# Ten units of the second filter group ahead of the mixer, and its later steps on an even grid

## The chip, the cores and the metric

The kernel runs on one core of one Trainium2 chip. The metric is the device time of one execution in microseconds (us), taken as the median over runs.

## The reference, cut to what matters

The input `x` has 8 batches of 3008 rows and 256 channels, in fp32. A filter is applied to every channel by a Fourier transform along the rows, and a token and channel mixer follows:

```python
X = np.fft.rfft(x, axis=1)
Y = X * (filt_r + 1j * filt_i)[None, :, :]
x = np.fft.irfft(Y, n=3008, axis=1)
h = np.maximum(x.transpose(0, 2, 1) @ w_tok1, 0.0) @ w_tok2     # 3008 -> 256 -> 3008
u = x + h.transpose(0, 2, 1)
out = u + np.maximum(u @ w_ch1, 0.0) @ w_ch2                    # 256 -> 1536 -> 256
```

The four mixer weights arrive as 64-bit floats and are converted on the chip.

## The kernel before, in words

The length 3008 is 47 x 64, so the Fourier transform is done as matmuls of length 64, a stage of length 47 with the filter in between, and the inverse.

**The filter.** `dft(bs)` is a generator for a group of batches; every `next()` puts one small piece of work into the program. The groups are `((0,), (1, 2), (3, 4), (5, 6), (7,))`. A group's steps are, in order:

- One step that only loads x tiles ahead (not in the first group). `x_load` (L397) fetches a tile of 128 partitions x 2 x 256 with two DMAs on SP's queue. From the second group on the tiles come from a pool of two buffers, `xp`.
- The length-64 units, `a_unit` (L415): 12 per batch, so 24 for a group of two. Each is a matmul of 128x512 (run as two passes, L417), a copy by ScalarE into `t1` (L422, two buffers) and a DMA of 256 KB to `z_tmp` on ScalarE's queue (L423). Behind each unit the load of the tile two units later is put into the program. In the first group the result stays on the chip: it is copied into `turned` (L419), and 16 VectorE transposes (L455) then turn its rows.
- Two steps without computation. The first of them loads the first chunks of `z_tmp` (`t2_load`, L457), filter and tables (`w_load`).
- The 33 length-47 steps (L515 on). Step k runs `b_unit(k)` (a matmul, L470, then the filter's products on VectorE, L482 to L486) and `bi_unit(k - 1)` (a matmul with the products, L494, a copy, L500, and after each second one a DMA to `g_tmp`, L505). For the first group, `filt_double` (L223) copies half of a filter tile on ScalarE, and `b_unit` reads it.

A unit's or step's PSUM bank is one of two, `acc` and `b`, taken by `free_bank`; the mixer's token sums and `u_part` use the same two.

**The weights.** `convert()` (L384) advances three queues over a list of weight tiles: the DMA of one tile, a ScalarE pass of the one before, and VectorE (or VectorE and PE, L284 and L285) for the one before that.

**The mixer.** `mix` (L703) goes over 8 batches x 36 items (6 column blocks m of 512 x 6 parts jp). In each item it runs the up matmuls (`up_first` L597, `up_last` L613), VectorE sums, the down matmuls of the item before (L631), and yields at three places, 0, 1 and 2. Items with jp 3 and 4 also run a `u_part` of the next block (L557, L562), between places 1 and 2. After each block, `finish` puts VectorE sums into the next items; they fall into items with i % 6 of 0, 1 and 2. Item 32 holds the token sums of the next batch (L540), which read `g_tmp` through `t4` (L534).

**The order.** It is written out by hand: every engine works through its own instructions in the order of the program, and SP and ScalarE also issue DMAs in that order. The first group's filter runs first, with conversions between its steps. The second group's generator (`second`) is advanced five times before the first mixer: once at the first group's step k == 25 (only x loads), twice in the loop over the remaining conversions, and twice right before `mix`. Its remaining steps are put at the places of the first mixer's 36 items by the condition at L835: while length-64 units remain, at places 1 and 2 of items 0 to 3 and at all three places from item 4 on; afterwards at place 1 of every item and at place 2 of odd ones. Later groups use place 1 alone. When the group ends (`done`), the loads of the next batch's `t4` go out.

Of the kernel before, what the change touches and what calls it, by code (L numbers as in the profile page):

```python
# [24 lines left out]
K2 = 32  # L25
# [4 lines left out]
NXC = A // XC  # L30
# [15 lines left out]
PARTS = (0, 64, 112)  # L46
BY_PE = 6
EARLY = 12
GROUPS = ((0,), (1, 2), (3, 4), (5, 6), (7,))


# [73 lines left out]
def kernel(  # L125
# [49 lines left out]
    def bank(tag):  # L175
        return (psg if tag == "pg" else psum).tile([P, 512], FP32, tag=tag, name="ps_" + tag)
# [114 lines left out]
    def w1_load(i):  # L291
        st = stage(512)
        rows = moe_w_tok1.rearrange("(n2 n1) t -> n2 n1 t", n1=N1)
        q = nc.sync if i < EARLY else nc.gpsimd
        last = 2 * i + 2 == A
# [88 lines left out]
    def convert():  # L384

        ended[0] += 1
        while behind and behind[0][0] < ended[0] - 2:
            behind.pop(0)[1]()
        advance(end)
        advance(copy)  # L390
        advance(begin)
# [139 lines left out]
    def t4_load(b, c, lo=PARTS[0], hi=P):  # L531
        if lo == 0:
            t4[b, c] = t4p.tile([P, TC4, D], FP32, tag="t4", name="t4")
        nc.sync.dma_start(t4[b, c][lo:hi], rows_of(g_d, b)[lo:hi, ts(c, TC4), :])  # L534
# [9 lines left out]
    def token_relu(acc):  # L544
        h1 = h1p.tile([P, TC, D], FP32, tag="h1", name="h1")
        nc.scalar.activation(out=h1, in_=acc, func=AF.Relu)
        return h1

    def width(m):
        return 512 if m < MT - 1 else 448  # L550
# [37 lines left out]
    def h_sums(hh, t, w):  # L588

        h = hh[:, :, 0:w // 2]  # L590
        return sums(t[:, :, 0:w // 2], h[:, 1:3], h[:, 0:2], h[:, 0], h[:, 3])

    def up_first(jp, ut, vt, w, g):
        hw = w // 2
        for ps, n, mov in ((g[0][:, 0], 0, ut[:, 0, 0:hw]), (g[0][:, 1], 5, vt[:, 2, 0:hw]),
                           (g[1][:, 0], 6, vt[:, 0, 0:hw]), (g[1][:, 1], 4, vt[:, 1, 0:hw])):
            nc.tensor.matmul(ps[:, 0:hw], chan[0][:, jp, n, :], mov, start=True, stop=True)  # L597

        s = sp.tile([P, 3, 256], FP32, tag="s", name="s")[:, :, 0:hw]
        nc.scalar.copy(out=s[:, 0], in_=g[0][:, 0, 0:hw])  # L600
        return s

    def up_middle(hh, w, g, s):
        hw = w // 2
        u2 = hh[:, 2, 0:hw]
        v(u2, g[0][:, 1, 0:hw], s[:, 0])
        v(s[:, 1:3], g[1][:, :, 0:hw], u2.unsqueeze(1).to_broadcast([P, 2, hw]))
# [74 lines left out]
    def u_part(b, m, dh):  # L682
        if dh == 0:
            uts[b, m] = up.tile([P, DH, 512], FP32, tag="u", name="u")
        u_unit(b, m, h1s[b], uts[b, m], dh)
# [13 lines left out]
    def one_step():  # L699
        if todo_v:  # L700
            todo_v.pop(0)()

    def mix(next_ready):  # L703

        wait = []
        pos, hhs, tts = {}, {}, {}

        def loads(b):
            if b + 1 < B and next_ready(b):
                for c in wait:  # L710
                    t4_load(b + 1, c)
                wait.clear()

        items = [(b, m, jp) for b in range(B) for m in range(MT) for jp in range(JP)]
        n = MT * JP
        for i in range(len(items) + 1):
            now, old = i < len(items), i >= 1
            convert()
            if now:
                b, m, jp = items[i]  # L720
                if i % n == 0:
                    wait.append(0)
                w = width(m)
                hhs[i] = hp.tile([P, 4, 256], FP32, tag="hh", name="hh")
                g = [bank("pg").rearrange("p (s n) -> p s n", s=2) for _ in range(2)]
                s = up_first(jp, uts[b, m], vts[b, m], w, g)
                up_middle(hhs[i], w, g, s)
            one_step()
            if old:
                bo, mo, jo = items[i - 1]  # L730
                tts[i - 1] = tp.tile([P, 4, 256], FP32, tag="t", name="t")
                for f in h_sums(hhs[i - 1], tts[i - 1], width(mo)):
                    f()
                down(mo, jo, 0, hhs[i - 1], tts[i - 1], pos.setdefault((bo, mo), []))
            yield b, i % n, 0
            convert()
            if now:
                up_last(jp, uts[b, m], vts[b, m], w, g, s, hhs[i])
            one_step()
            loads(b)  # L740
            yield b, i % n, 1
            if old:
                down(mo, jo, 1, hhs.pop(i - 1), tts.pop(i - 1), pos[bo, mo])
                if jo == JP - 1:
                    todo_v.extend(finish(bo, mo, uts[bo, mo], pos[bo, mo]))
                    one_step()
                    one_step()
            if now:
                if m + 1 < MT and jp in (3, 4):
                    u_part(b, m + 1, jp - 3)  # L750
                    if jp == 4:
                        wait.append(m + 1)
                        todo_v.extend(v_steps(b, m + 1))
                if b + 1 < B:
                    j = i % n - n
                    if j == -4:
                        h1s[b + 1] = token_relu(token_sums(b + 1))
                    elif j == -3 or j == -2:
                        u_part(b + 1, 0, j + 3)
                        if j == -2:  # L760
                            todo_v.extend(v_steps(b + 1, 0))
            loads(b)
            yield b, i % n, 2
        while todo_v:
            one_step()

    with tc.manual_schedule():
        nc.sync.dma_start(wa0, wa0_d)
        nc.vector.memset(turned[:, A:K2, :], 0.0)
        for t in filts:  # L770
            nc.vector.memset(t, 0.0)
        rounds = 0
        second = dft(GROUPS[1])
        for i, _ in enumerate(dft(GROUPS[0])):
            if i == 0:
                for t, src in ((wai_t, wait_d), (wa, wa_d), (wai, wai_d), (ident, ident_d)):
                    nc.scalar.dma_start(t, src)

            if i < NXC:
                if i in (0, 2, 4, 6):  # L780
                    advance(begin)
                if i == 5:
                    advance(copy)
                if i in (7, 9, 11):
                    convert()
                    rounds += 1
            else:
                if (i - NXC) % 3 == 2:
                    convert()
                    rounds += 1  # L790

                k = i - NXC - 2
                if 19 <= k < 25:
                    t4_load(0, k - 19, 0, PARTS[1])
                elif k == 25:
                    next(second)
                elif k in (30, 31):
                    for c in range(3):
                        t4_load(0, 3 * (k - 30) + c, PARTS[1], PARTS[2])
        for c in range(A // TC4):  # L800
            t4_load(0, c, PARTS[2], P)
        sum_up()
        both = wcp.tile([P, 2, JP, 7, P], FP32, tag="wc", name="wc")

        chan.extend((both[:, 0], both[:, 1]))
        for i in range(rounds, A // 2 + TC * N2 // NG):
            convert()
            if i - rounds < XB:
                next(second)
            if i == A // 2 + BY_PE - 1:  # L810
                sum_up()
                acc = token_sums(0)
        h1s[0] = token_relu(acc)
        for dh in range(DH):
            convert()
            u_part(0, 0, dh)
        for f in v_steps(0, 0):
            f()
        for _ in range(XB):
            next(second)  # L820
        group, todo, done = -1, iter(()), True

        def next_ready(b):
            return done or b != GROUPS[group][-1]

        for b, i, place in mix(next_ready):
            if group + 1 < len(GROUPS) and b == GROUPS[group + 1][0]:
                if not done:
                    raise AssertionError("the filter's steps don't fit beside the mixer's")
                group += 1  # L830
                done = group + 1 == len(GROUPS)
                todo = iter(()) if done else dft(GROUPS[group + 1]) if group else second
                spread = True

            if not done and (place == 1 or group == 0 and (spread and (place == 2 or i > 3) or place == 2 and i % 2)):  # L835
                spread = next(todo, "end")
                done = spread == "end"

# [29 lines left out]
```

## Time and profile before

| | |
|---|---|
| Median of 6 runs | 2587.64 us (2586.78 to 2590.57) |
| Profiled execution | 2589.03 us |
| Its span | 2587.0 us |
| PE, matmuls | 2505.7 us busy, 97% |
| VectorE (DVE) | 1815.3 us, 70% |
| ScalarE (ACT) | 691.1 us, 27% |
| GpSimd (POOL) | 526.7 us, 20% |
| DMA | 205.20 MB, mean 79 GB/s |

The page lists busy time by engine, then 40 slices of the span in which a digit is the busy share in tenths, then DMA queues, the chain of waits that ended last, and the costliest groups of instructions. In the timeline a row is: start, duration, engine, line, operation, output<-inputs, count, and in brackets the idle time of the engine before it with what ended it. `SPq` and `ACTq` are the queues that issue DMAs. PE is the matmul engine, PEld its weight loads. In the windows view each row is a stretch of time with the busy time of every engine in it.

### The profile page before, as it was taken

The page shows a single profiled execution, that of the slowest core. Times are in us where ns is not written, and L with a number is a line of the kernel's source. Part 1 is how long each engine was busy: PE and PEld are TensorE (multiplying, and loading weights), DVE is VectorE, ACT ScalarE, POOL GpSimd, SP SyncE. Part 2 cuts the span into 40 slices and gives each one's busy share as a digit, 9 for nine tenths or more (in the row PEclk, how much of TensorE's full clock was granted, in tenths as well). Part 3 has the DMA queues.
Part 4 walks back from the last instruction along what each step waited for, and adds up shares of the span by engine and source line. Part 5 has one row for each costly group of instructions (what it writes and reads, how often), then busy time and mean ns, then how long its engine had stood idle before and what let it go on. Part 6 is the DMA issues. An engine that isn't in the chain of part 4 may idle for free.

```text
span 2587.0 us, 31459 instructions
## 1 busy us (share of the span) xinstructions
PE 2505.7 (97%) x10952; PEld 2001.9 (77%) x10952; DVE 1815.3 (70%) x3458; ACT 691.1 (27%) x1347; POOL 526.7 (20%) x966
## 2 busy tenths in 40 slices
PE   5979999999999999999999999999999999999998
PEld 2556766788878777888787777788888888888887
DVE  6897888556675888746666788846678577647676
ACT  2433222123221222222321222212222122212222
POOL 3653211111211112112112111121121121211212
PEclk7999999999999999999999999999999999999999
DMA  6964333312232332202232223211232121100001
GB/s 167 232 195 154 109 106 103 106 48 90 90 90 63 88 88 72 80 17 89 90 96 77 75 84 87 80 31 57 90 85 75 50 64 53 25 9 8 17 12 21
DMA packets 151835, 205.20 MB, mean 79 GB/s; under 512 B 34217, under 2 KB 102035, under 8 KB 151677
## 3 DMA queue, kind: packets, MB, share of 16 engines
q1 hardware_dynamic: 81068, 115.65, 15.3%
q0 software_dynamic: 30656, 39.93, 6.4%
q10 hardware_dynamic: 39952, 47.61, 5.7%
q8 instruction: 87, 1.43, 0.2%
q14 instruction: 72, 0.58, 0.1%
HBM read 131.23 MB, written 71.83 MB: 78 GB/s over the span
## 4 chain that ended last, share of the span: by engine, by line
PE 80%; DVE 12%; DMA 2%; issue 2%; ACT 2%; POOL 0%; SPq 0%; ACTq 0%; DVEq 0%; POOLq 0%
PE ps_po L631 27%; PE ps_pg L597 16%; PE ps_pg L613 12%; PE ps_b L540 4%; PE ps_b L557 4%; DVE t L575 2%; PE ps_acc L540 2%; PE ps_acc L557 2%; DVE hh L575 2%; PE ps_acc L494 2%; PE ps_b L562 2%; PE ps_acc L417 2%; PE ps_b L470 1%; DVE u L575 1%; PE ps_b L494 1%
## 5 line engine op out<-in xcount | busy, mean ns | idle before, releaser
L575 DVE TENSOR_TENSOR hh<-ps_pg,s 128x512 f32<-128x512 f32 (+3 forms) x864 | 482.0, 585 | 624.4 <-ACT s L600 623.8
L676 POOL DMA_DIRECT2D out_dram<-r x757 | 409.8, 550 | 1948.4 <-ACT hh L618 928.3
L618 ACT ACTIVATE hh<-hh 128x512 f32<-128x512 f32 (+1 forms) x576 | 347.9, 621 | 1121.4 <-DVE hh L575 1121.4
L631 PE MATMUL ps_po<-t,wc 128*128 128x256 f32 (+1 forms) x2304 | 535.5, 375 | 5.3 <-DVE t L575 4.6
L631 PEld LDWEIGHTS ps_po<-t,wc 128*128 128x128 f32 x2304 | 434.5, 190 | 132.8 <-issue 53.3
L631 PE MATMUL ps_po<-hh,wc 128*128 128x256 f32 (+1 forms) x1728 | 413.2, 375 | 2.9 <-POOL wc L339 2.5
L597 PE MATMUL ps_pg<-v,wc 128*128 128x256 f32 (+1 forms) x1728 | 413.4, 375 | 0.3
L631 PEld LDWEIGHTS ps_po<-hh,wc 128*128 128x128 f32 x1728 | 327.5, 190 | 41.8 <-POOL wc L339 2.9
L597 PEld LDWEIGHTS ps_pg<-v,wc 128*128 128x128 f32 x1728 | 326.9, 190 | 40.6 <-DVE v L575 3.0
L613 PE MATMUL ps_pg<-u,wc 128*128 128x256 f32 (+1 forms) x1152 | 294.3, 378 | 7.0 <-DVE hh L575 6.5
L575 DVE TENSOR_TENSOR t<-t,hh 128x256 f32<-128x256 f32 (+1 forms) x576 | 242.0, 420 | 19.8
L613 PEld LDWEIGHTS ps_pg<-u,wc 128*128 128x128 f32 x1152 | 216.3, 190 | 43.1 <-DVE hh L575 16.8
L575 DVE TENSOR_TENSOR s<-ps_pg,hh 128x512 f32<-128x512 f32 (+1 forms) x288 | 196.1, 681 | 30.7 <-DVE hh L575 0.9
L575 DVE TENSOR_TENSOR t<-hh 128x512 f32<-128x512 f32 (+1 forms) x288 | 192.6, 669 | 0.6 <-ACT hh L618 0.6
L597 PE MATMUL ps_pg<-u,wc 128*128 128x256 f32 (+1 forms) x576 | 170.0, 377 | 3.6 <-DVE hh L575 3.6
L613 PE MATMUL ps_pg<-v,wc 128*128 128x256 f32 (+1 forms) x576 | 169.2, 375 | 0.0
L600 ACT COPY s<-ps_pg 128x256 f32<-128x256 f32 (+1 forms) x288 | 106.0, 368 | 154.7 <-PE ps_pg L597 151.5
L597 PEld LDWEIGHTS ps_pg<-u,wc 128*128 128x128 f32 x576 | 102.5, 191 | 22.1 <-issue 8.9
L613 PEld LDWEIGHTS ps_pg<-v,wc 128*128 128x128 f32 x576 | 108.9, 190 | 13.4
L540 PE MATMUL ps_b<-t,w 128*128 128x256 f32 x480 | 106.1, 383 | 4.0 <-DMA t<-g_tmp 4.0
L557 PE MATMUL ps_b<-w,h 128*128 128x512 f32 (+1 forms) x232 | 107.8, 587 | 0.0
L540 PEld LDWEIGHTS ps_b<-t,w 128*128 128x128 f32 x480 | 92.1, 192 | 17.5 <-ACT both L245 3.7
(102 smaller groups left out, 2252.6 us busy)
## 6 DMA issues: line engine op xcount, KB each, us to landing
g_tmp<-t ACTq DMA_DIRECT2D x128, 192.0 KB
x<-in_x_dram SPq DMA_DIRECT2D x184, 128.0 KB
out_dram<-r POOLq DMA_DIRECT2D x698, 32.0 KB, 1.8
z_tmp<-t ACTq DMA_DIRECT2D x84, 256.0 KB
t<-z_tmp SPq DMA_DIRECT2D x112, 192.0 KB
t<-g_tmp SPq DMA_DIRECT2D x42, 512.0 KB
wb<-wbi_t SPq DMA_DIRECT2D x80, 224.0 KB
filt<-in_filt_r_dram SPq DMA_DIRECT2D x128, 48.0 KB
```

What stands on the lines that cost most here:

```text
L417: nc.tensor.matmul(ps, wa0 if b == 0 else wa, xs.pop((b, c)).rearrange("p a d -> p (a d)"), start=True, stop=True)
L494: nc.tensor.matmul(ps[0:KR], wbs[k // WC][:, k % WC, P:], p, start=(i == 0), stop=(i == len(parts) - 1))
L540: nc.tensor.matmul(acc[:, t, :], w1[:, a, ts(t, P)], t4[b, a // TC4][:, a % TC4, :], start=(a == 0 and t == 0), stop=(a == A - 1 and t == ...
L557: nc.tensor.matmul(ps[:, 0:w], h1[:, t, ts(dh, P)], w2[:, t, ds(m * 512, w)], start=(t == 0), stop=False)
L562: nc.tensor.matmul(ps[:, ds(q * P, n)], t4[b, c][:, r, ts(dh, P)], wai[:, 0:n], start=False, stop=(q == 3))
L575: nc.vector.tensor_tensor(out=out, in0=in0, in1=in1, op=op)
L597: nc.tensor.matmul(ps[:, 0:hw], chan[0][:, jp, n, :], mov, start=True, stop=True)
L600: nc.scalar.copy(out=s[:, 0], in_=g[0][:, 0, 0:hw])
L613: nc.tensor.matmul(ps[:, 0:hw], chan[0][:, jp, n, :], mov, start=True, stop=True)
L618: nc.scalar.activation(out=hs, in_=hs, func=AF.Relu)
L631: nc.tensor.matmul(po[i][:, j, 0:hw], chan[1][:, jp, n, :], mov, start=(jp == 0 and first == 1), stop=(jp == JP - 1 and last == 1))
L676: q.dma_start(rows[g, e, :, ds(h * A + 4 * m, n)], blocks[ts(g, CW), h, e, 0:n])
```

## The change

A constant `AHEAD = 10` is added. In the first group's loop, the step of `second` that only loads x tiles moves from k == 25 behind the tenth length-64 unit (i == 9), and after the twelfth and last one (i == 11) ten of the second group's length-64 units are put into the program. The first group's generator puts its VectorE transposes into the program when it is advanced next, that is behind these ten units. The two advances in the conversion loop and the two ahead of `mix` stay, so ten units of 24 are left for the first mixer instead of 20.

In the first mixer the remaining units take places 1 and 2 of every item, place 0 no longer. The 35 steps that follow (2 + 33, `K2 + 3`) are spread over 52 places, two per item over 26 items: a step falls on a place where the whole part of `at * left / places` goes up.

```diff
+AHEAD = 10
 GROUPS = ((0,), (1, 2), (3, 4), (5, 6), (7,))
...
                 if i in (7, 9, 11):
                     convert()
                     rounds += 1
+                if i == 9:
+                    next(second)
+                if i == NXC - 1:
+                    for _ in range(AHEAD):
+                        next(second)
...
                 if 19 <= k < 25:
                     t4_load(0, k - 19, 0, PARTS[1])
-                elif k == 25:
-                    next(second)
                 elif k in (30, 31):
...
+        left, places, at, spread = K2 + 3, 2 * 26, 0, True
         for b, i, place in mix(next_ready):
...
                 todo = iter(()) if done else dft(GROUPS[group + 1]) if group else second
-                spread = True
-
-            if not done and (place == 1 or group == 0 and (spread and (place == 2 or i > 3) or place == 2 and i % 2)):
+            due = place == 1
+            if group == 0 and place:
+                due = spread
+                if not spread:
+                    at += 1
+                    due = at * left // places > (at - 1) * left // places or at > places
+            if due and not done:
                 spread = next(todo, "end")
                 done = spread == "end"
```

## The prediction

> **What bounds the kernel now.** I read the page's slices first, then the timeline around the transposes, then the windows view with borders that I chose from the timeline.
>
> ```profile
> PE 2505.7 (97%) x10952; PEld 2001.9 (77%) x10952; DVE 1815.3 (70%) x3458; ACT 691.1 (27%) x1347; POOL 526.7 (20%) x966
> PE   5979999999999999999999999999999999999998
> PEclk7999999999999999999999999999999999999999
> DMA  6964333312232332202232223211232121100001
> ```
>
> PE is the bound, except in the first slices (65 us each). There the timeline shows one hole:
>
> ```profile
> 31.53 17.01 DVE L455 STREAM_TRANSPOSE turned<-turned 128x512 f32<-128x512 f32 x16 [1.86 <-ACT turned L419]
> 32.37 1.92 PE L285 MATMUL ps_po<-both,wai_t 128*128 128x512 f32 x2
> 48.64 1.19 PE L470 MATMUL ps_b<-turned,wb 128*128 128x256 f32 x2 [14.36 <-issue]
> 49.93 0.42 DVE L482 TENSOR_TENSOR p<-ps_b,filt 128x256 f32<-128x256 f32 x1 [1.39 <-issue]
> ```
>
> While VectorE transposes for 17.01 us, PE stands idle for 14.36 us. Windows, here on the clock's own grid of 3.41 us (columns: length, busy time of PE, PEld, DVE, ACT, POOL, granted clock, DMA share, GB/s):
>
> ```profile
> 14.39:17.80 3.41, 1.10 (x2) 0.30 (x2) 0.00 (x0) 1.00 (x2) 1.32 (x3) 1.00 1.04 243
> 17.80:21.22 3.42, 2.31 (x3) 1.12 (x4) 2.24 (x4) 0.91 (x3) 0.00 (x0) 0.50 1.06 253
> 34.87:38.28 3.41, 0.00 (x0) 0.00 (x0) 3.41 (x4) 1.23 (x3) 0.00 (x0) 1.00 1.05 229
> 38.28:48.60 10.32, 0.00 (x0) 0.00 (x0) 10.26 (x10) 0.00 (x0) 0.00 (x0) 0.50 0.17 39
> ```
>
> The DMA engines are full until about 40 us, and empty only behind that. PE's clock halves after a window with PE busy for 1.10 of 3.41 us, and stays halved through windows with 2.31 busy. Now the same view with one line per item of the first mixer (border: the first L597 matmul on u; items 4, 5, 6, 8, 12, 13, 17):
>
> ```profile
> 214.60:226.40 11.80, 11.49 (x47) 8.19 (x46) 8.11 (x16) 4.38 (x8) 4.62 (x10) 1.00 0.41 135
> 226.40:235.30 8.90, 8.90 (x36) 6.40 (x35) 5.20 (x10) 3.25 (x7) 0.00 (x0) 1.00 0.54 171
> 235.30:244.20 8.90, 8.79 (x35) 6.36 (x34) 5.20 (x10) 3.62 (x7) 0.00 (x0) 1.00 0.55 180
> 253.90:259.90 6.00, 6.00 (x29) 5.29 (x28) 4.27 (x8) 1.44 (x3) 0.00 (x0) 1.00 0.40 130
> 290.90:298.60 7.70, 7.70 (x33) 5.98 (x32) 7.42 (x14) 2.73 (x5) 0.00 (x0) 1.00 0.33 100
> 298.60:310.20 11.60, 10.21 (x37) 6.46 (x36) 11.33 (x22) 2.44 (x5) 0.00 (x0) 1.00 0.37 110
> 341.40:351.90 10.50, 9.69 (x38) 6.65 (x37) 8.73 (x16) 2.65 (x5) 0.00 (x0) 1.00 0.26 79
> ```
>
> A bare item takes 6.04 us, all PE. Item 12 has one length-47 step: 7.76, that is 1.72 per step and no stall. Items 5 and 6 hold three length-64 units each and PE is full. Items 13 and 17 hold two steps (9.48 of work) and take 11.6 and 10.5. Items 0 to 3 (167.9 to 214.6) last 10.2 to 12.6 us with DVE busy 9.8 to 11.9: the weights' conversions bind there, not PE.
>
> **Part 1: ten units leave the mixer.** Items 0 to 3 keep two units each, so nothing changes there. Items 4 to 7 held three each, now two in item 4 and none later: ten gone, from items where PE is 8.8 of 8.9 us busy. A unit is two matmuls of 128x512; items of the second mixer with one unit take 6.90 against 6.04, so 0.86 each. Ten are **-8.6 us** (bounds -6 and -8.6, if DVE keeps part of item 4).
>
> **Part 2: ten units enter the gap.** Their PE time is free there; what costs is that PE takes them in order ahead of the first b_unit. Each unit needs its x tile (two DMAs of 128 KB on SP), and xp has two buffers, so x_load(n+2) waits for unit n. The round trip in the trace: a load issued at 549.21 on quiet queues has its last landing at 552.50, 3.3 us. Under load the one issued at 248.31 (three DMAs) let PE start at 252.93, 4.6 us; in the saturated stretch the chain of waits shows 5.21 us (issue 23.48). In the gap only z writes (256 KB per unit) run beside it, so I take 3.35, near the quiet row, and keep 5.21 as the other end.
>
> SP issues the first two loads behind the stage loads of 28.16 to 29.3; the engines drain these at about 1.1 us per 256 KB until 36.2, so x 0 is usable at 37.4 and x 1 at 38.5. PE is free at 34.3, so it waits. Unit 0 ends at 38.5, unit 2 starts at 41.9. From there a pair of units costs 3.35 + 0.1 + one unit. The window 34.87 to 38.28 will hold under 1 us of PE work, less than the 1.10 that halved the clock at 17.80, so a unit takes 1.9 (the L285 pair above), and the pair 5.35. Unit 8 starts at 41.9 + 3 x 5.35 = 58.0, unit 9 ends at 61.4, or 60.9 with a window or two granted in full. ScalarE then copies it (0.59), issues its z write (0.35) and only then doubles the first filter (0.62), which the first L482 needs: 62.5 instead of 49.93, **+12.6 us**. Queued behind: on PE all b_units and the on-chip sums, on ACT the filter copy, on SP the third wb load and the next w_tok1 tile (both wanted over 8 us later). VectorE stands idle from 48.5. From here to the mixer everything is a chain of PE, ACT and DVE steps, so the delay is carried on.
>
> The Trainium skill speaks on the clock ("TensorE: Matmul & The Clock Gate", Part 1: The HAM clock gate): as it has it, throttling comes after an idle window, and a busy one releases it. The row at 14.39 differs: that window was a third busy and was followed by 0.50. By the page the units would keep full speed once warm, pairs would take 4.4 us and the delay be 9.4; by the rows it is 12.6, and the rows decide.
>
> **Part 3: the loads that move from step 25.** The first next(second) was at k == 25:
>
> ```profile
> 103.13 4.02 SPq L406 DMA_DIRECT2D x<-in_x_dram  x4
> 111.97 0.62 ACT L225 COPY filt<-filt 64x512 f32<-64x512 f32 x1 [4.41 <-DMA filt<-in_filt_r_dram]
> ```
>
> These 0.5 MB go out at a DMA share near 1, and right after them filters come late. Steps take 6.1 to 6.7 us per three until 110.4; the last three take 10.7 instead of 6.1 (110.4 to 121.1): 4.6 lost, part of it at half clock. The 0.5 MB are 2.1 us of transfer at 246 GB/s; with the clock I take **-3.0** (0 to -4.6).
>
> **Part 4: the spread.** The rule becomes 35 steps over the 52 places of items 5 to 30. Written out, floor(35 n / 52) gives four steps per three items, with the double always in the middle one: items 7, 10, 13, 16, 19, 22, 25, 28, 30. So doubles do not vanish, they move. Stalls today, period less 6.04, 1.72 per step and 2.61 per u_part: items 13, 19, 25 (with finish's sums on DVE) 2.1, 2.5, 2.1; items 11, 17, 23, 29 (second step waits for the first one's products) 1.0 to 1.1 each; items 15, 21, 27 (bank held by a u_part's copy) 0.9 each; item 10 0.5, items 5 to 7 1.6, item 31 0.5: together 16.4. After: 13, 19, 25 and now 7: 8.7; 10, 16, 22, 28 like 15: 3.8; item 30: 1.1; item 31 0.5: 14.1. The lone steps at place 2 are not in this trace; DVE needs 1.1 + 2.7 us there before up_middle, and PE has 4.7 us of work queued, so I take nothing. **-2.2** (-5 to +2). The second group also ends half an item earlier, so the wait of the next token sums for t4 (0.83 at 495.92) goes: **-0.8** (0 to -1.4).
>
> **Sum.** 12.6 - 8.6 - 3.0 - 2.2 - 0.8 = -2.0. The profiled execution took 2589.03 (span 2587.0, 2.0 around it), 1.4 above the median of 2587.64; it would become 2587.0, the median **2585.6**.
>
> **Rivals.** *Faster by over 0.2%:* the units run at full clock, as L417 does in the mixer (1.02 a unit, so 3.35 + 0.1 + 1.0 = 4.4 a pair; unit 8 at 55.2, unit 9 over at 57.7, delay 9.4), and the loads' removal gives back all 4.6: 9.4 - 4.6 - 11.6 = -6.8, so 2580.8. For it: unit 2 and 3 together fill the window of 41.7 to 45.1, which can release the clock. Against: the next ones, waiting for x, leave it under half busy again. *Slower:* the x round trip in the gap. Four trips lie on the path to unit 8, so each us more costs 4. At the saturated row, 5.21, the delay is 12.6 + 4 x 1.86 = 20.0 and the sum +5.4: 2593.0; it decides from 5.15 up. For it: ten loads and ten z writes are 5.2 MB, 21 us of a full DMA system. Against: at 5.35 us a pair they ask for 1 MB per pair, 196 GB/s, below the 246 that the trace reached. *Not what it says:* the spread is not more even where it counts (doubles on all finish items); that is in the forecast, and if the lone steps at place 2 also stalled like doubles (1.0 each, eight of them), the sum would be +6, against which stands DVE's slack there.
>
> **How the numbers follow.** 0.2% (5.2 us) is about what a measurement of this kernel can tell from no change. Within it, with the terms as taken: 0.54. Faster: 0.26. Slower, by the round trip 0.14 and by the lone steps 0.06: 0.20. The range reaches to both rivals' prices and leaves out a tenth on each side: 2579 to 2593; the likeliest case alone spans 2582 to 2590.
>
> **What would show it.** Right: L417 matmuls on wa from about 37 us on in pairs 5 to 5.5 us apart with waits on x, at half clock; the first L470 at 61; the step of L225 at 107 without its 4.41 wait; the first item at about 177.5 instead of 167.9; items 5 at 6.0, 13 still at 11.6; mixer 2 beginning about 2 us before 537.9. Wrong: a first L470 before 57 or after 66, items 4 to 7 not shorter by 8, or lone-step items over 8 us.

## The result and the profile after

The changed kernel takes 2597.21 us (median of 14 runs, 2591.02 to 2601.5) against 2589.0 for the kernel before in the runs taken beside it: a ratio of 1.0031, 95% interval 1.0024 to 1.0038. The forecast was 2585.6 with a range up to 2593.0; the kernel is slower, by 8.2 us. The profiled execution took 2597.29 us with a span of 2595.1. Line numbers after the constant are higher by one (L417 is now L418, L470 is L471, L482 is L483), and by a few more in some runs below. The page, busy times and the slices of 65 us:

```profile
PE 2510.8 (97%) x10952; PEld 2003.8 (77%) x10952; DVE 1815.0 (70%) x3458; ACT 691.3 (27%) x1347; POOL 526.0 (20%) x966
...
PE   5988999999999999999999999999999999999998
PEclk7999999999999999999999999999999999999999
DMA  7874233312232222203232232211222121100001
```

The instruction counts are those of before, and PE is still 97% busy; only the order of the same work differs. The slices are too coarse to show the gap: the first stays at 5, the third goes from 7 to 8, the fourth from 9 to 8. The timeline of the changed kernel shows what that work does to the gap (start, duration, instruction, and in brackets the idle time ahead of it):

```profile
38.33 2.04 PE L418 MATMUL ps_b<-x,wa 128*128 128x512 f32 x2 [4.20 <-DMA x<-in_x_dram]
...
44.84 2.05 PE L418 MATMUL ps_b<-x,wa 128*128 128x512 f32 x2 [2.76 <-DMA x<-in_x_dram]
...
63.74 2.05 PE L418 MATMUL ps_b<-x,wa 128*128 128x512 f32 x2 [2.25 <-DMA x<-in_x_dram]
...
67.30 0.60 PE L471 MATMUL ps_b<-turned,wb 128*128 128x256 f32 x2
...
69.29 0.42 DVE L483 TENSOR_TENSOR p<-ps_b,filt 128x256 f32<-128x256 f32 x1 [19.88 <-ACT filt L226]
```

Before, PE waited 14.36 us for VectorE and the first b_unit ran at 48.64. Now VectorE waits 19.88 us: its transposes end at 49.4, but the ten units hold PE until 67.30. Each even unit waits for its x tile; the pairs start 6.4 to 6.5 us apart, the last one 6.0. One round of the chain of waits of the changed kernel (start, duration, what) gives the price of that wait:

```profile
40.40 0.47 SPq L407
...
40.91 3.79 DMA x<-in_x_dram
...
44.84 2.06 PE ps_b L418 x2
```

The load is issued the moment unit 0 has freed its buffer, takes 0.5 us to issue and 3.79 us to land, and the matmul starts 4.44 us after the issue; the next trips take 4.36, 4.38 and 3.92. The windows view, first the whole stretch of the units, then items 4, 5, 13, 16 and 17 of the first mixer (columns as in the prediction):

```profile
36.46:67.18 30.72, 18.45 (x20) 5.88 (x21) 12.95 (x13) 5.27 (x9) 0.00 (x0) 0.50 0.51 162
...
232.50:244.30 11.80, 10.67 (x45) 7.74 (x44) 8.12 (x16) 3.81 (x8) 4.61 (x11) 1.00 0.28 86
244.30:250.40 6.10, 6.10 (x30) 5.34 (x29) 4.29 (x9) 1.47 (x4) 0.00 (x0) 1.00 0.47 164
...
314.50:326.50 12.00, 10.33 (x37) 6.39 (x36) 11.70 (x23) 2.21 (x5) 0.00 (x0) 1.00 0.31 95
344.60:357.70 13.10, 12.43 (x51) 8.53 (x51) 7.12 (x12) 3.35 (x6) 0.00 (x0) 1.00 0.13 37
357.70:365.80 8.10, 8.02 (x34) 5.93 (x32) 7.77 (x15) 2.18 (x4) 0.00 (x0) 1.00 0.39 116
```

Item 5 is a bare item as forecast (6.1). Item 4 still takes 11.80 although PE has 0.82 us less to do in it. A double in an item with a `u_part` takes 13.1, one with `finish`'s sums 12.0, a lone step at place 2 takes 8.1 in item 17. All 30.72 us of this stretch ran at half clock.

Between borders of the program, the forecast and the traces stand like this (us, after less before):

| stretch | forecast | measured |
|---|---|---|
| start to the first filter product (49.93, 69.29) | +12.6 | +19.4 |
| from there to the last length-47 step (121.1, 136.4) | -3.0 | -4.1 |
| from there to the first token sums (137.5, 155.85) | 0 | +3.0 |
| from there to the first item (167.9, 186.3) | 0 | +0.1 |
| the first mixer's items up to batch 1 (537.9, 546.1) | -11.6 | -10.2 |
| sum | -2.0 | +8.2 |

Within the mixer, from the first up matmul of one item to that of the next, items 4 to 31 take 266.3 us in place of 273.8, item 32 takes 26.0 in place of 28.3, and items 0 to 3 take 46.2 in place of 46.8. All later batches take the same time in both.

### The profile page after: what moved, and what is told of

Same layout as the page of the kernel before. It is cut to its first block, busy times and chain, and to the rows that moved or that the text cites. A ratio compares the mean times of both kernels' runs of the same rounds, so it can differ in the third digit from the quotient of the medians.

```text
span 2595.1 us, 31463 instructions
## 1 busy us (share of the span) xinstructions
PE 2510.8 (97%) x10952; PEld 2003.8 (77%) x10952; DVE 1815.0 (70%) x3458; ACT 691.3 (27%) x1347; POOL 526.0 (20%) x966
## 4 chain that ended last, share of the span: by engine, by line
PE 81%; DVE 12%; DMA 2%; issue 2%; ACT 2%; POOL 1%; SPq 0%; ACTq 0%; DVEq 0%; POOLq 0%
PE ps_po L632 28%; PE ps_pg L598 16%; PE ps_pg L614 12%; PE ps_acc L558 4%; PE ps_b L541 3%; PE ps_acc L541 3%; PE ps_b L558 2%; DVE t L576 2%; PE ps_acc L495 2%; DVE hh L576 2%; PE ps_acc L563 2%; PE ps_b L418 2%; PE ps_b L471 2%; DMA x<-in_x_dram 2%; PE ps_acc L471 1%
## 5 line engine op out<-in xcount | busy, mean ns | idle before, releaser
L576 DVE TENSOR_TENSOR s<-ps_pg,hh 128x512 f32<-128x512 f32 (+1 forms) x288 | 196.1, 681 | 30.7 <-DVE hh L576 0.9
L558 PE MATMUL ps_acc<-w,h 128*128 128x512 f32 (+1 forms) x232 | 107.6, 587 | 0.7 <-ACT h L547 0.7
L495 PE MATMUL ps_acc<-p,wb 128*96 128x256 f32 (+1 forms) x256 | 94.5, 468 | 10.7 <-DVE p L487 5.2
L541 PE MATMUL ps_b<-t,w 128*128 128x256 f32 x384 | 85.6, 386 | 7.4 <-issue 6.1
```

The costliest lines, as they stand in the source:

```text
L495: nc.tensor.matmul(ps[0:KR], wbs[k // WC][:, k % WC, P:], p, start=(i == 0), stop=(i == len(parts) - 1))
L541: nc.tensor.matmul(acc[:, t, :], w1[:, a, ts(t, P)], t4[b, a // TC4][:, a % TC4, :], start=(a == 0 and t == 0), stop=(a == A - 1 and t == ...
L558: nc.tensor.matmul(ps[:, 0:w], h1[:, t, ts(dh, P)], w2[:, t, ds(m * 512, w)], start=(t == 0), stop=False)
L576: nc.vector.tensor_tensor(out=out, in0=in0, in1=in1, op=op)
```

## The experiments

Two theories stood against each other. **The round trip**: the units behind the second wait for their loads, whose trip beside the z writes takes 4.4 us, so each pair costs 6.5 us in the gap and saves only 1.7 in the mixer. **The units themselves**: ten units at half clock are 19 us of PE work, so that any unit put here costs about 1.9 whatever the loads do. Beside these, the new grid of steps could have cost something.

**Four units instead of ten (`ahead4`).** The 35 steps are spread over 47 places from item 8 on. The last of them falls on item 31, as in the kernel before, and not on item 30, as in the change.

```diff
-AHEAD = 10
+AHEAD = 4
...
-        left, places, at, spread = K2 + 3, 2 * 26, 0, True
+        left, places, at, spread = K2 + 3, 2 * 24 - 1, 0, True
```

> Four units in the gap instead of ten (AHEAD = 4), 16 left for the first mixer (two per item to item 7), the 35 steps over 47 places from item 8 on. Theory (round trip: units 0 and 1 find their tiles loaded, every further pair waits for an x load and costs 6.5 us): unit 3 ends at about 48.6 as in the changed kernel, so the first L470 stays at 48.6 to 49.5 and the delay is under 1.5 us; four units fewer in PE-bound items; 2584 to 2588. Rival (any unit in the gap pushes the first L470 back by its share, 1.9 us each): first L470 at 56, time 2592 or more.

2585.23 us against 2588.79, ratio 0.9988 (0.998 to 0.9997). Its timeline:

```profile
47.82 1.19 PE L471 MATMUL ps_b<-turned,wb 128*128 128x256 f32 x2 [0.56 <-issue]
```

The four units start at 36.9, 38.7, 43.5 and 45.3 and are over before the transposes are: the first b_unit comes at 47.8, no later than before, and the first filter product follows the last transpose by 1.39 us, as before. The units left the mixer for nothing: items 4 to 7 take 35.1 us instead of 39.2. Part of that is lost again, since the same 35 steps on this even grid make items 8 to 31 longer (237.0 instead of 234.6), and item 32 stays at 28.2. All this speaks against a price per unit, and shows that the change was right in kind and too large: two pairs fit into the time of the transposes, five do not. (The moved loads are in this kernel too; `load_only` below shows what they are worth alone.)

**Ten units with more x tiles (`six_tiles`).** The tiles rotate over three pools of the same size that are unused then, and six are loaded ahead.

```diff
-        where, tag = ((xp, "x"), (tp, "t"), (vp, "v"))[c % 3] if b == 0 else (xp, "x")
+        where, tag = ((xp, "x"), (tp, "t"), (vp, "v"))[c % 3] if b == 0 or (b == 1 and c < 10) else (xp, "x")
...
-        ahead = 3 * XB if first else XB
+        second_ = bs[0] == 1
+        ahead = 3 * XB if first or second_ else XB
...
```

> Ten units in the gap as in the change, but their x tiles rotate over six buffers (xp, tp, vp), so loads run ahead. Theory (round trip on two buffers): the pairs 6.5 us apart vanish, units follow one another at 1.7 to 2.1 us, the first L470 moves from 67.3 to 55 to 59, time about 10 us under the changed kernel, 2585 to 2589. Rival (the gap is bound by DMA throughput or by the z writes, not by the tiles): first L470 stays above 64, time above 2594.

2588.28 us, ratio 0.9997 (0.9988 to 1.0005): 9 us of the loss are gone. The first b_unit is at 60.2, 7.1 earlier than in the change, not 8 to 12 as expected. The timeline shows the limits that took over:

```profile
48.51 1.26 PE L418 MATMUL ps_acc<-x,wa 128*128 128x512 f32 x2 [2.95 <-ACT t L423]
...
59.00 1.45 PE L418 MATMUL ps_acc<-x,wa 128*128 128x512 f32 x2 [2.57 <-DMA x<-in_x_dram]
60.24 1.06 PE L476 MATMUL ps_b<-turned,wb 128*128 128x256 f32 x2
```

Units 0 to 4 run 1.3 to 1.7 us apart. Unit 5 then waits 2.95 us for a bank, which ScalarE has yet to copy into one of the two `t1` buffers; these come free with the z writes (the copy of unit 3, at 47.88, waits 3.49 us for one). Unit 9 waits for a load again. The clock rose as well (1.00 from 43.28 to 46.70), so the 7.1 us are not the tiles' alone. The first limit was the x tiles, and behind it stands the way out of a unit, bank and `t1`.

**The load step alone (`load_only`, from the kernel before).**

```diff
+                if i == 9:
+                    next(second)
...
-                elif k == 25:
-                    next(second)
```

> Kernel before with one edit: the step that only loads x tiles moves from k == 25 to i == 9. No unit in the gap, old places. My forecast's part 3: the last steps lose their wait for filters and the time falls by 3.0 us. What the changed trace suggests instead: steps finish 3.4 us earlier, but the first token sums' loads (t4) are bound by DMA work behind them and give back about 3.0, so the time falls by 0 to 1 us.

2587.93 us, ratio 0.9995 (0.9986 to 1.0003). The length-47 steps take 69.3 us instead of 72.5, as forecast, though a second execution of the kernel before needs only 71.1; the stretch behind them up to the token sums takes 17.8 instead of 16.4. What arrives at the end can't be told from zero.

**The change with the old rule for the steps (`gap_old_grid`).**

```diff
             if group == 0 and place:
                 due = spread
                 if not spread:
-                    at += 1
-                    due = at * left // places > (at - 1) * left // places or at > places
+                    due = place == 1 or i % 2 == 1
```

> The change with the old rule for the 35 steps (place 1 always, place 2 in odd items), from item 5 on. It tells what the even grid is worth. My count of stalls per double step: 15.9 us here against 14.1 with the grid, so 1 to 2 us slower than the changed kernel, 2597 to 2600. Rival (the spread itself costs, by its lone steps at place 2): 1 to 4 us faster than the changed kernel.

2597.35 us, ratio 1.0035 (1.0021 to 1.0049). From the first item to batch 1 it takes 359.7 us, the change 359.8, and in both items 4 to 31 take 266.3. The even grid is worth nothing: neither the forecast's gain of 2.2 nor a loss.

**No z writes in the gap (`late_z`).** The ten units do not write their tiles; as many writes are done in a later group, with that group's tiles in their place.

```diff
-        nc.scalar.dma_start(rows_of(z_d, b)[:, ts(c, XC), :], t1)
+        if b != 1 or c >= AHEAD:
+            nc.scalar.dma_start(rows_of(z_d, b)[:, ts(c, XC), :], t1)
+        if b == 2 and c < AHEAD:
+            nc.scalar.dma_start(rows_of(z_d, 1)[:, ts(c, XC), :], t1)
```

> The change, but the ten units of the gap write nothing to z_tmp there; the same rows are written later from the tiles of batch 2 (so batch 1 is filtered from wrong rows; the work is the same, in another place). Theory (the z write beside each x load stretches the round trip from 3.3 to 4.4 us): pairs 5.3 to 5.5 us apart instead of 6.5, first L470 at 62 to 64 instead of 67.3. Rival (a pair of loads takes 4.4 us in any case when it is waited for): first L470 stays at 66.5 to 68.

One execution, 2593.95 us; first b_unit at 62.2. The same round of its chain of waits:

```profile
39.63 0.47 SPq L407
...
40.13 2.73 DMA x<-in_x_dram
...
43.00 2.04 PE ps_b L418 x2
```

The load lands in 2.73 us instead of 3.79, and the trip is 3.4 us, the quiet figure that the forecast had used. So it is the writes of 256 KB, running beside the two loads of 128 KB, that add the 1.06 us, though the DMA engines are only half busy in the mean (0.51 in the row above). Of the 5.1 us by which the first b_unit comes earlier, 3.9 are the four trips (13.2 us instead of 17.1) and 0.8 is the first tile. The clock also rose in two windows (0.95 in 46.70 to 50.11 and in 56.94 to 60.35).

**Filler matmuls (`warm`).** Two matmuls of 128x512 on data that is there anyway stand ahead of every pair, into a bank that nothing reads.

```diff
-                    for _ in range(AHEAD):
+                    for n in range(AHEAD):
+                        if n % 2 == 0:
+                            idle = bank("pg")
+                            for _ in range(2):
+                                nc.tensor.matmul(idle, wa, filts[1][:, 0].rearrange("p k d -> p (k d)"),
+                                                 start=True, stop=True)
                         next(second)
```

> The change with two extra 128x512 matmuls into a free bank before every pair of units, only to keep PE busy. Theory (the half clock adds about 1.0 us to each pair's path): the clock is granted in full through the gap, pairs come 5.4 us apart instead of 6.5, first L470 at 62 to 64. Rival (the clock is nothing there, the loads are all): pairs stay 6.5 apart or grow by the extra matmuls, first L470 at 67 or later.

One execution, 2593.1 us; first b_unit at 63.9, 3.4 earlier than in the change. The windows view over the same stretch:

```profile
36.46:67.18 30.72, 23.01 (x48) 8.54 (x47) 14.59 (x16) 7.50 (x14) 0.00 (x0) 0.94 0.65 201
```

With more to do PE kept its clock (0.94 in place of 0.50), and the pairs come 5.0 to 5.4 us apart behind a first distance of 6.35. So the clock is a part of the loss: 3.4 us, where leaving out the z writes gained 5.1 and more tiles 7.1. The three overlap and can't be added.

The Trainium skill ("TensorE: Matmul & The Clock Gate", "HAM oscillation — how this bites in real kernels") gives as a rule to have no PE idle time above some 3.4 us. In the change the clock fell before that: at 36.46, 2.3 us into the first wait (4.20 us long). The waits behind it, 2.25 to 2.76 us, kept to the rule, and the clock still stayed at 0.50, with PE busy for 18.45 of 30.72 us. Here the measurement decides. What brought the clock back was a window of the 3.41 us grid with PE busy throughout; one with 2.61 us busy did not:

```profile
56.94:60.35 3.41, 2.61 (x3) 1.12 (x4) 0.00 (x0) 0.53 (x1) 0.00 (x0) 0.50 0.40 149
...
63.76:67.18 3.42, 3.42 (x4) 1.29 (x5) 0.00 (x0) 0.58 (x1) 0.00 (x0) 0.50 0.30 108
67.18:70.59 3.41, 3.29 (x11) 1.61 (x9) 1.26 (x3) 2.14 (x4) 0.00 (x0) 1.00 0.85 280
```

**Four units and steps at chosen places (`ahead4_places`).** Doubles at places 0 and 2 of the items with i % 6 of 3, 4 and 5, single steps at place 1 of the others, to keep doubles out of the items with `finish`'s sums.

```diff
-AHEAD = 10
+AHEAD = 4
...
-            if group == 0 and place:
...
+            if group == 0:
+                due = place > 0 if spread else place in ((0, 2) if i % 6 in (3, 4, 5) else (1,))
```

> Four units in the gap, and another grid for the 35 steps from item 8 on: place 1 in items with i % 6 of 0, 1 and 2, places 0 and 2 in those with 3, 4 and 5. So no double falls on a finish item and the two steps of an item lie 3 us of other work apart. If the stalls per double are as counted (second step waits for the first one's products, VectorE full on finish items), 24 items lose about 10 us less than in ahead4: 2574 to 2580. If a double costs the same wherever it lies: 2584 to 2587.

2581.32 us (6 runs, 2578.2 to 2582.67), ratio 0.997 (0.9958 to 0.9982): faster than both kernels, by less than expected. Items 10 to 13 in the windows view:

```profile
263.40:276.40 13.00, 12.32 (x49) 8.45 (x48) 9.69 (x16) 2.77 (x5) 0.58 (x2) 1.00 0.28 79
276.40:285.90 9.50, 9.50 (x37) 6.72 (x36) 9.19 (x17) 2.15 (x5) 0.00 (x0) 1.00 0.47 127
285.90:294.50 8.60, 7.98 (x33) 5.80 (x32) 8.30 (x15) 3.27 (x8) 0.00 (x0) 1.00 0.34 100
294.50:303.30 8.80, 8.29 (x34) 5.86 (x33) 8.58 (x19) 1.81 (x5) 0.00 (x0) 1.00 0.22 63
```

The double of i % 6 == 5 has lost its stall: 9.50 us, all of it PE. The one of i % 6 == 4 still takes 13.0, and the single steps behind the doubles now stall (8.60 and 8.80 in place of 7.8). Items 8 to 31 take 235.1 us against 237.0 in `ahead4`, and item 32 takes 26.0 against 28.2, since the last step falls on item 30 here and on item 31 there. Together that is 4.1 us, about what lies between the two medians (3.9). The profiled executions differ elsewhere too: the first mixer begins 2.7 us later here.

**Five units, each with a tile of its own (`ahead5_tiles_places`).** The grid is that of `ahead4_places`.

```diff
-AHEAD = 10
+AHEAD = 5
...
-        where, tag = ((xp, "x"), (tp, "t"), (vp, "v"))[c % 3] if b == 0 else (xp, "x")
+        where, tag = ((xp, "x"), (tp, "t"), (vp, "v"))[c % 3] if b == 0 or (b == 1 and c < AHEAD) else (xp, "x")
...
-        ahead = 3 * XB if first else XB
+        ahead = 3 * XB if first else AHEAD if bs[0] == 1 else XB
...
```

> Five units in the gap with a tile each (xp, tp, vp), so none waits for an x load, with the grid of ahead4_places. Theory (only units that wait for a load delay the first L470): first L470 at 47 to 49.5, one unit less in the mixer, 0.5 to 1.5 us under ahead4_places. Rival (the fifth unit pushes the first L470 back as well): first L470 at 50 or later, time as ahead4_places or over it.

2582.52 us, ratio 0.9972 (0.996 to 0.9983), the same as with four. Its timeline:

```profile
48.85 1.19 PE L474 MATMUL ps_b<-turned,wb 128*128 128x256 f32 x2 [3.12 <-DVE turned L459]
```

The first b_unit comes at 48.9, 1 us later than with four, but not for the fifth unit: that one is over at 45.7, and PE waits 3.12 us for the transposes, which begin 1.0 us later in this execution (31.56; 31.53 and 32.02 in the kernel before). So with a tile each a fifth unit fits into the gap, as the theory had it. It makes items 4 to 7 shorter by 0.8 us, but item 31 takes 9.3 instead of 7.8, and nothing is left of it at the end.

**The chosen places alone (`places_only`, from the kernel before).**

```diff
-            if not done and (place == 1 or group == 0 and (spread and (place == 2 or i > 3) or place == 2 and i % 2)):
+            due = place == 1
+            if group == 0:
+                due = place == 1 or place == 2 or i > 3 if spread else place in ((0, 2) if i % 6 in (3, 4, 5) else (1,))
+            if due and not done:
```

> The kernel before with only the grid of ahead4_places for the 35 steps (no unit in the gap, load at k == 25). It parts the gain of ahead4_places. From the item borders, the grid is worth 2.2 us at item 32 and 0 to 2 in the items, the gap's four units 3 to 4: so 2584 to 2587 here. If the grid did all of it: 2580 to 2582.

2588.15 us, ratio 0.9998 (0.9989 to 1.0007). The grid alone does not show. Items 8 to 31 take 235.1 us, against 234.6 in the kernel before, since the doubles' stalls moved to the items behind them; item 32 got shorter (26.0 instead of 28.3), and items 4 to 7 took 1.0 longer. So the chosen places are better than the even grid of `ahead4`, but not than the old rule; what `ahead4_places` gains on the kernel before lies in items 4 to 7 (4.2 us) and in item 32 (2.2).

**Repeats, for the scatter between executions.** `before_again`, `after_again` and `load_again` are the kernel before, the change and `load_only`, unchanged.

> The kernel before, profiled once more, to see how much the stretch from the last length-47 step of the first group to the first token sums varies (16.4 us in its first profile, 19.4 in the changed kernel's). If the 3.0 us are a price of the change: 16.0 to 16.8 again. If they are scatter of a stretch that is bound by DMA: anything from 15.5 to 19.5.

> The changed kernel, profiled once more. First L470 at 66.5 to 68 either way. If the 3.0 us behind the last step are a price of the change: 19 to 20 us again. If they are scatter: 15.5 to 19.5.

> The kernel load_only, profiled once more. First to last step 69 to 70 us (72.5 in the kernel before) if the moved load is what ended the filters' wait there; last step to token sums 15.5 to 19.5 if that is scatter, 17.5 to 18.1 if not.

2590.04, 2601.96 and 2584.06 us. The first b_unit of the change is at 69.1 this time, later than expected: the first tile comes 1.1 us later, and the four trips take 4.56, 4.39, 4.40 and 4.48 us. What was read from the gap holds. The stretch from the last length-47 step to the token sums scatters. In the windows view of the kernel before and of the change:

```profile
121.10:137.50 16.40, 12.75 (x39) 6.38 (x38) 12.37 (x29) 10.43 (x19) 3.30 (x6) 0.99 1.01 237
```

```profile
136.40:155.80 19.40, 12.81 (x39) 6.42 (x37) 15.67 (x36) 11.01 (x20) 3.89 (x7) 0.92 1.04 253
```

PE has the same 12.8 us of work in both, with the DMA engines full. The kernel before takes 16.4 and 18.0, `load_only` 17.8 and 15.6, the change 19.4 and 19.1, `gap_old_grid` 18.7, `ahead4_places` 18.6, `ahead5_tiles_places` 18.0, `ahead4` 15.9, and `places_only` 13.1. `six_tiles`, `late_z` and `warm`, which also have ten units in the gap, take 16.3, 16.1 and 17.4. One program differs from itself by up to 2.2 us here, and between the kernel before and the change lie 1.1 to 3.0, by which executions one takes. So the +3.0 in the table is in part scatter and doesn't come with the ten units as such; how much of it the change causes stays open.

## Why the prediction was wrong, point by point

**Part 2, the gap: this step failed.** The mechanism was right (pairs of units, each waiting for its loads, at half clock, with all b_units behind them), the sizes were not. The delay exceeds 12.6 by 6.8 us. Of these, 3.3 are the round trip: from issue to matmul, four trips of 4.44, 4.36, 4.38 and 3.92 are 17.1 us, where the forecast has four of 3.35 + 0.1. I had named the z writes as what runs beside the loads and still taken the row of the quiet queues; `late_z` shows that 3.4 holds only without these writes. The other end was not measured alike either: 5.21 is a landing alone, 1.16 us after the issues of that load began (22.32), while 3.35 has the issue in it. Another 1.9 are unit 0: its tile came at 38.3 rather than 37.4, and it ran at half clock (2.04, not 1.1). Units 2, 4 and 6 held their buffers for 2.1 rather than 1.9 each, which makes 0.5. The rest, 1.1, is behind the fourth trip: the last pair got no window at full clock, and the first product followed its matmul by 2.0 rather than 1.6.

**Part 1, the units out of the mixer: nearly right.** Items 5 and 6 became bare items. The unit that left item 4 gave nothing: the last unit of that item waits 1.13 us for its bank, which ScalarE has to empty, and the item stays at 11.8 us. That lies within the bounds given, and costs 0.86 of the value taken.

**Part 3, the loads: right where it was read, not seen at the end.** The steps got shorter by 3.4 in the change and by 3.2 in `load_only`, or by 2.0 and 1.8 against the second execution of the kernel before. The largest wait for a filter that is left there is this one of the changed kernel's timeline, where the old one was 4.41:

```profile
129.58 0.62 ACT L226 COPY filt<-filt 64x512 f32<-64x512 f32 x1 [2.54 <-DMA filt<-in_filt_r_dram]
```

What failed is the assumption that the gain is carried on: the stretch behind it is full of transfers and takes as much more or less as it happens to (15.6 or 17.8 in one and the same program).

**Part 4, the spread: no gain of 2.2.** Taken one by one, the stalls after the change were right (12.0 and 13.1 for the doubles, against 11.6 and 13.0), but lone steps at place 2 of i % 6 == 5 stall by 0.36 each (the other four not at all; the rival had 1.0 for all eight), and `gap_old_grid` reaches the same time from the first item to batch 1 with the old rule. Together with Part 1, items 4 to 31 gained 7.5 us of 10.8. The wait for the next token sums did go, and with more than the 0.8 taken: item 32 gained 2.2, 0.75 of it work that was moved ahead. In all, the mixer gained 10.2 of the 11.6; that it came so near is partly luck, as the surplus of item 32 and 0.6 in items 0 to 3 make up for the grid.

**The rivals.** The slower one named the right mechanism, the x round trip. Its point of decision, 5.15 us, was wrong: it was reckoned with every other term as forecast. At the measured trips the sum would still be only +1.3; unit 0, the rest of the gap, the stretch ahead of the token sums and the mixer's shortfall did the rest (1.9, 1.6, 3.0 and 1.4, less 1.1 that the steps gave more). The case of a full clock had nearly the price that `warm` shows: 3.4 us on the first b_unit, where the two forecasts for the gap differ by 3.2. As the added matmuls shift the loads too, that is partly luck. For its condition it looked to a window filled by units 2 and 3; they ran without a break for 3.75 us, but across two windows of the grid (1.86 and 1.89 us busy), and the clock stayed at 0.50. All three signs of "wrong" came: a first L470 after 66 (67.3), items 4 to 7 shorter by 4.3 us and not by 8, with a double now in item 7, and lone-step items over 8 us (8.1).

## What to carry to other kernels

Work moved into an idle gap is free only as far as its buffers reach: count how many pieces fit before the gap's owner is done, at the period of a buffer's round trip, and move that many. Here that was four units of ten with two tiles (a pair past that costs 6.5 us in the gap and saves 1.7), and it turned a loss of 0.3% into a gain of 0.1%, or 0.3% together with steps whose places cost less than the even grid's and which end one item earlier. Take the round trip of a load from a row in which the same writes run beside it, not from the quietest row.

## What was not expected of the hardware

- Writes of 256 KB beside two loads of 128 KB lengthened the loads' landing from 2.73 to 3.79 us, at a mean DMA share of 0.51. A mean share well below 1 does not say that a dependent load is undisturbed.
- PE busy for 60% of a stretch of 30.7 us, with no wait above 2.8 us behind the first unit, did not bring back the full clock; with 75% (`warm`) the mean clock was 0.94. Keeping it took less than regaining it: in `warm` a window of 3.41 us at full clock with PE busy for 1.93 us was followed by full clock (35.71 to 39.12), and one with 0.95 us by half (42.54 to 45.95).
- 3.75 us of PE work without a break did not bring it back either where a border of the 3.41 us windows cut it in two (1.86 and 1.89 us); 3.42 us within one window did, and 2.94 in `late_z` (53.18 to 56.60).
